# Eleven of 26 convolution groups as float32 tap sums on GpSimd and VectorE, in a dilated attention and gated convolution kernel with a written-out order

## The chip, the cores and the metric

The kernel runs on one core of one Trainium2 chip. The metric is device time in microseconds (us), the median of several runs. A profile of one execution stands beside the times: its span runs from the first to the last instruction, and the execution's own time is a little longer than its span. Engines: PE (TensorE, matmul; PEld is its weight load), DVE (VectorE), ACT (ScalarE), POOL (GpSimd), SP (SyncE, which issues the DMAs).

## The reference, cut to what matters

Sliding attention in two kinds of heads, then a gated unit with a causal convolution of five taps along the sequence:

```python
# attention: 8 batches x 8 heads x 576 positions x 64; heads 0-3: the 32 last positions,
# heads 4-7: every fourth of the 128 last
x = attn_out.transpose(0, 2, 1, 3).reshape(B, S, H * D)        # 8 x 576 x 512
for k in range(K):                                             # K = 5
    gate_pre += conv_w[k][None, None, :] * xp[:, k:k + S, :]   # xp: x with 4 zeros ahead
gate = 1.0 / (1.0 + np.exp(-gate_pre))
out = (gate * (x @ w_val)) @ w_out
```

## The kernel before, in words

Everything is cut into tasks, each a few instructions of one engine. `Plan.add` makes a task with its dependencies and the buffers it holds; `ORDER` (lines 16 to 50) lists all task numbers in the order in which they are emitted, with a letter for the engine (P, A, V, G for GpSimd, S) and, behind it, a number of dummy matmuls ("heat", line 659) to be put ahead of that task. `HOMES` gives the buffer number of each buffer use. Nothing is scheduled at run time: each engine does its tasks in that order, and waits for what it needs from others.

A batch goes through these steps. `Lq`, `Lk`, `Lv` load q, k, v (`p` for the plain heads, `d` for the dilated). `Tq`, `Tk` transpose on PE (lines 401, 464), `Eq`, `Ek` copy out of PSUM to qT and kT (312 on ACT, 314 on DVE, both in the helper `copy`). `S` multiplies the scores (333), `E` takes the exponential on ACT (340), `M` multiplies by the mask on DVE (347), both its inputs in SBUF. `A` multiplies by v (356), `N` divides by the sum on DVE (365, 366). `X` transposes back on PE (428, 488) and `F` copies into xT (312, 314), which holds a pair of batches with channels on the partitions, in four chunks of 128; the plain heads give chunks 0 and 1, the dilated heads chunks 2 and 3. GpSimd (316) casts v to bf16: `U` the dilated v (vn, one cast of 128x1536), `HA` to `HD` the plain v of the first four batches (vw, 2, 3, 3 and 2 casts), and once `Wv` and `Wo` the weights (w_val, w_out), whose float32 copies come in by DMA in the three buffers wt0 to wt2.

The gated unit works on pairs of batches, g = 0 to 3. A pair's 1152 tokens are cut in three blocks of 384 (the middle one spans both batches), in the last pair in four of 288; a block has two halves of two channel chunks, cp = 0 and 1. That makes 26 groups, named by g, block k and cp: group 111 is pair 1, block 1, chunks 2 and 3. Each group has a convolution `C` (line 530: 20 matmuls of 64x64 diagonal weights, one for each of five taps, two chunks and two halves of the partitions, summing in PSUM), the tanh `G` on ACT (540), the value product `V` (548, eight matmuls), and the product `Y` of both on DVE (558) into yT. The convolution of a second chunk of a group exchanges the upper and lower 64 partitions (line 528), and the weights are laid out for that. Output blocks `O` of 128 tokens (577, four matmuls) follow when the products of their tokens are there, `EO` evicts them (584 on ACT, 586 on DVE), `ST` stores them.

GpSimd's casts end with the fp32 weights; after about 70 us it has only three casts of vn left. In `homes` and `run` it is asserted that a buffer isn't used by two tensors at once, in the order as written.

Of the kernel before, what the change touches and what calls it, by code (L numbers as in the profile page):

```python
# [7 lines left out]
FP32 = mybir.dt.float32  # L8
BF16 = mybir.dt.bfloat16
AF = mybir.ActivationFunctionType  # L10
ALU = mybir.AluOpType
# [10 lines left out]
135P 185P 136A 125P 128P 129A 126A 111V 165P 166A 140V 130V 137V 116G 127V 186V 234S 202S 157P 158A 187P 115G
118G 117G 141P 171S 175P 176A 188V 192P 193A 131P 142V 132V 173P 172G 174A 189P 190A 208P 209V 210A 143P 133P
177P 178A 180P 203S 134V 211P 235S 250P 144V 159P 181A 213A 212A 227P 228A 153P 154A 11S 238P 205G 251V 194V
179V 191V 160V 182V 239A 206A 195P 229V 196V 207A 167P 168V 204G 12G 183P 184V 155P 252P 224P 225A 214P 240P
215A 9S 253V 156V 199P 254P 241V 255A 226V 217P 218A 161P 230P 197P 162A 200A 324S 267S 236S 216V 219V 245P
256V 220P 198A 246A 231V 10G 625P 628P 221V 323S 266S 325S 237G 626A 257P 242P 243A 276P 629A 222P 326G 223A
258A 278A 277V 163P 341P 232P 303P 247V 244V 259V 233V 342V 304A 299P 300A 164V 339P 260P 248P 329P 305P 330A
340V 268S 261V 631P 630S 355S 384S 533S 627S 346P 356S 249V 343P 264P 306V 265V 273P 632A 347A 344A 348V 274V
275A 272A 345V 262P 301P 302V 279P 280A 292P 634P 635V 263A 349P 350V 327P 293A 328A 289P 281V 282P 283A 290A  # L30
284V 271G 270G 269G 643P 644A 637P 285P 291V 294V 400P 401V 286V 638A 334P 331P 335A 332A 336V 640P 641A 295P
388P 389A 358P 296V 360A 311P 312A 361P 363A 333V 359V 287P 362V 288V 297P 337P 298A 338V 385S 417S 374P 375A
319P 386S 320A 307P 308A 353P 351P 639S 377P 364P 354V 376V 313P 357S 469S 642S 416S 352A 378A 379V 365A 402P
321P 390P 314V 403V 407P 367P 322V 649P 366V 368A 391A 380P 309P 485P 408A 650A 381V 369V 310V 404P 392P 393A
405A 486V 646P 370P 647A 422P 419P 394V 371V 424V 423A 421A 645S 470S 651S 633S 502S 418S 655P 382P 438P 409V
395P 420A 439A 387G 396A 315P 316A 449P 656A 383V 406V 410P 652P 411V 450A 435P 531S 425P 372P 653A 436A 426A
440V 397V 373V 317P 658P 654S 530S 532S 471S 451P 487P 501S 318V 427V 437V 659A 473P 441P 488A 452V 398P 475P
442V 445P 399V 476A 447P 446A 474A 492P 493A 428P 661P 429A 448V 494V 430V 548P 549V 472G 489P 480P 507P 662A
490A 491V 536P 537V 481A 508A 443P 444V 660S 663S 565S 657S 564S 509A 431P 432V 482V 550P 551A 477P 478A 412P
504P 555P 413A 556A 479V 433P 434V 505A 506A 495P 496V 414P 453P 454A 415V 552P 483P 484V 553A 538P 664P 539A  # L40
523P 510P 511A 524A 520P 521A 676P 570P 665V 497P 567P 677A 569A 568A 554V 557V 571A 636S 461P 462A 522V 525V
572A 534S 667P 463P 503S 498A 666S 648S 455P 535G 670P 671A 526P 464V 668V 456V 527V 566S 673P 558P 682P 559V
674A 672S 669S 678S 583P 586P 587A 584A 499P 588V 683V 500V 457P 458A 465P 466A 513P 585V 459P 460V 528P 589P
529A 514A 590V 679P 680A 691P 573P 540P 541A 576P 574A 577A 685P 515V 512V 692V 686A 516P 681S 684S 687S 517V
467P 591P 518P 605P 468V 519A 597P 606A 601P 578V 575V 592V 543P 602A 688P 579P 542V 544A 598A 580V 599P 689A
545V 603P 581P 582A 600V 546P 694P 547V 604V 695A 697P 698V 609P 593P 560P 562P 561V 563A 610A 594A 595P 675S
696S 690S 699S 703P 700P 704V 596V 701V 607P 608V 706P 709P 611P 612V 705S 702S 693S 621P 617P 710V 613P 622A
711S 707A 708S 715P 712P 716A 618A 713A 614A 615P 616V 714S 619P 623P 721P 722A 718P 719A 620V 624V 727P 717S
723S 720S 724P 728A 725A 729S 726S 730P 731A 732S
"""  # L50

HOMES = "01010210000113130211000021002000132000231120022230241102145110103141020101013010110671123222114010302002121011010121100020122020000113021121100010231011014002232122312230001402035111113121011000001040001271122022114211200220201210102211110120022006000113012301031011031312015002120122131011400020471110130403021302202101000612230101122001201213021121220010101202202400001311141011120300130017102102012110131140321053111213132000031220020210061030221022401013242000210112021202210011202120011203140201100102021003120310041312140112140011020113140211031200110403"
# [17 lines left out]
DEPTH = 5  # L70
NAT = 4
# [31 lines left out]
class Plan:  # L103
# [28 lines left out]
    def run(self):  # L132
# [4 lines left out]
        for word in order:  # L137
# [19 lines left out]
def kernel(  # L157
# [10 lines left out]
    nc = tc.nc  # L168
# [13 lines left out]
    NCH = Dm // 128  # L182
# [39 lines left out]
    conv_w = consts.tile([128, NCH, K], BF16, name="conv_w")  # L222
# [82 lines left out]
    SHIFTS = (("HA", ((1, 0, 64, 64, 0), (1, 64, 64, 0, 1)), 1.0),  # L305
# [196 lines left out]
    def gated(g, xb, w_ready):  # L502
# [3 lines left out]
        for k in range(n_blk):  # L506
# [14 lines left out]
            for cp in range(2):  # L521
                pc, gt, pv = Ten("ps2"), Ten("gate"), Ten("ps2")

                def conv(eng, cp=cp, pc=pc, c0=c0, mov=mov, dst=dst, wd=wd):
                    for kk in range(K):
                        for n in range(2):
                            for hb in range(2):
# [7 lines left out]
                t_c = plan.add(f"C{g}{k}{cp}", (PE,), conv,  # L535
                               deps=[x_done[(b, 2 * cp + n)] for b in last for n in range(2)] + [w_ready["conv"]],
                               tens=[pc, gt, xb], out=pc)

                def th(eng, pc=pc, gt=gt, wd=wd):
                    nc.scalar.activation(out=gate[gt.idx][:, :, 0:wd], in_=ps2[pc.idx][:, :, 0:wd],  # L540
                                         func=AF.Tanh, scale=0.5)
                t_g = plan.add(f"G{g}{k}{cp}", (ACT,), th, deps=[t_c], tens=[pc, gt])

                def val(eng, cp=cp, pv=pv, c0=c0, mov=mov, dst=dst, wd=wd):
                    for n in range(2):
# [163 lines left out]
```

## Time and profile before

| | us |
|---|---|
| median of 3 runs | 174.27 |
| lowest, highest | 173.8, 174.28 |
| the profiled execution, its own time | 173.37 |
| its span | 171.7 |

The profile's rows are read thus. A group of instructions stands as line, engine, operation, out<-in by the program's names, partitions x elements and type, count; behind the bar the busy time in us and the mean ns of one, behind the second bar the idle time of the engine just before them and what ended it. The timeline has start, length, engine, line and operation. A window's row has the stretch and its length, then each engine's busy time with its number of instructions. The view of one line or tile has the shortest, median and longest duration in ns. The chain that ended last is followed back from the last instruction, at each step to what released it.

### The profile page before, as it was taken

To read this page: it belongs to the slowest core of one execution; us is meant where nothing else is said; L and a number is where in the kernel's file an instruction comes from. 1 tells how busy PE (TensorE), PEld (TensorE's weight loads), DVE (VectorE), ACT (ScalarE), POOL (GpSimd) and SP (SyncE) were. 2 spreads that over 40 slices of the span, in tenths; PEclk is the share of its full clock that TensorE was granted. 3 is DMA by queue.
4 is the path that set the end of the run, shared out by engine and by line. 5 is a ranking of instruction groups with operands and counts; after the bars stand their busy time and mean duration, and the time that the engine had idled before them with its cause. 6 is when DMAs were issued, how large, how long until landed. Compare 5 with 4: busy or idle time off the path is not lost.

```text
span 171.7 us, 5752 instructions
## 1 busy us (share of the span) xinstructions
PE 153.0 (89%) x2441; PEld 102.2 (60%) x2460; DVE 121.7 (71%) x243; ACT 108.4 (63%) x182; POOL 44.2 (26%) x82
## 2 busy tenths in 40 slices
PE   6697967888989979899999799989999999999990
PEld 1355654677557546567766567576656577666640
DVE  6549778989899579779788658899368776664220
ACT  2147976198868744798847693888946675242542
POOL 7023998560659427403000000210110000000000
PEclk9999999999999999999999999999999999999999
DMA  4999999999799999999994948969979060333445
GB/s 137 325 355 290 375 370 210 311 374 319 200 383 364 362 269 281 373 353 222 282 328 139 267 115 286 373 165 390 270 202 303 2 244 4 116 119 138 186 165 199
DMA packets 49123, 43.63 MB, mean 254 GB/s; under 512 B 22981, under 2 KB 39365, under 8 KB 49098
## 3 DMA queue, kind: packets, MB, share of 16 engines
q1 hardware_dynamic: 49098, 43.27, 82.2%
q8 instruction: 19, 0.31, 0.7%
q14 instruction: 6, 0.05, 0.1%
HBM read 33.83 MB, written 9.44 MB: 252 GB/s over the span
## 4 chain that ended last, share of the span: by engine, by line
PE 58%; DMA 12%; DVE 11%; ACT 6%; SPq 5%; issue 3%; POOL 3%; ACTq 0%; DVEq 0%; POOLq 0%
PE pu L577 17%; PE pd L548 14%; PE pd L530 9%; DMA qk<-in_k_dram 5%; PE pd L356 5%; DVE et L347 4%; DMA wt<-in_moe_w_out_dram 4%; SPq L281 4%; PE pd L333 4%; DMA qk<-in_q_dram 3%; PE pu L464 3%; POOL w_out L316 3%; PE pd L401 2%; PE pu L488 2%; ACT et L340 2%
## 5 line engine op out<-in xcount | busy, mean ns | idle before, releaser
L340 ACT ACTIVATE et<-pd 128x576 bf16<-128x576 f32 x64 | 39.3, 657 | 10.4 <-PE pd L333 9.3
L347 DVE TENSOR_TENSOR et<-et,mask 128x576 bf16<-128x576 bf16 x64 | 33.9, 557 | 4.7 <-ACT et L340 4.5
L548 PE MATMUL pd<-xT,w_val 128*128 128x384 bf16 (+1 forms) x208 | 34.9, 313 | 0.7 <-DVE xn L366 0.4
L577 PE MATMUL pu<-w_out,yT 128*128 128x512 bf16 x127 | 33.4, 379 | 1.4 <-issue 0.6
L558 DVE SCALAR_TENSOR_TENSOR yT<-gate,pd 128x768 bf16<-128x768 bf16 (+1 forms) x26 | 23.0, 886 | 12.5 <-PE pd L548 8.5
L366 DVE TENSOR_TENSOR xn<-pd,rec 96x768 bf16<-96x768 f32 x32 | 30.5, 954 | 1.1
L316 POOL CAST vn<-vd 128x1536 bf16<-128x1536 f32 x8 | 12.3, 1540 | 70.3 <-DMA vd<-in_v_dram 70.3
L540 ACT ACTIVATE gate<-pd 128x768 bf16<-128x768 f32 (+1 forms) x26 | 19.9, 769 | 10.9 <-DVE yT L558 5.5
L548 PEld LDWEIGHTS <-w_val 128*128 128x128 bf16 x208 | 19.4, 97 | 11.6 <-issue 1.5
L530 PE MATMUL pd<-xT,conv_diag 64*64 64x384 bf16 (+1 forms) x520 | 23.1, 313 | 1.8 <-DVE xT L314 1.1
L584 ACT ACTIVATE osb<-pu 128x512 f32<-128x512 f32 x27 | 16.2, 601 | 11.0 <-PE pu L577 10.7
L577 PEld LDWEIGHTS <-yT 128*128 128x128 bf16 x144 | 12.6, 97 | 13.3 <-issue 1.1
L333 PE MATMUL pd<-qT,kT 64*128 64x96 bf16 x384 | 16.1, 209 | 3.1 <-ACT qT L312 0.9
L530 PEld LDWEIGHTS <-conv_diag 64*64 64x64 bf16 x520 | 15.1, 106 | 6.2 <-issue 2.5
L316 POOL CAST vw<-vp 32x384 bf16<-32x384 f32 (+2 forms) x31 | 16.8, 541 | 7.5 <-DMA vp<-in_v_dram 6.1
L356 PEld LDWEIGHTS <-et 128*128 128x128 bf16 x384 | 14.7, 97 | 6.5 <-DVE et L347 2.5
L464 PE MATMUL pu<-ident,qk 128*128 128x128 bf16 x160 | 14.8, 230 | 3.0 <-DMA qk<-in_k_dram 2.0
L333 PEld LDWEIGHTS <-kT 64*128 64x128 bf16 x384 | 10.1, 96 | 11.5 <-issue 6.3
L464 PEld LDWEIGHTS <-qk 128*128 128x128 bf16 x160 | 10.8, 102 | 7.3 <-DMA qk<-in_k_dram 3.0
L314 DVE COPY xT<-pu 128x576 bf16<-128x576 bf16 x18 | 10.1, 568 | 4.0 <-PE pu L488 3.1
L312 ACT COPY xT<-pu 128x576 bf16<-128x576 bf16 x14 | 8.9, 646 | 6.2 <-PE pu L428 3.6
L365 DVE RECIPROCAL rec<-pd 96x12 f32<-96x12 f32 x32 | 7.1, 223 | 7.6 <-PE pd L356 4.5
(52 smaller groups left out, 146.2 us busy)
## 6 DMA issues: line engine op xcount, KB each, us to landing
out_dram<-osb SPq DMA_DIRECT2D x36, 256.0 KB, 2.7
vd<-in_v_dram SPq DMA_DIRECT2D x8, 768.0 KB, 9.3
qk<-in_k_dram SPq DMA_DIRECT2D x8, 576.0 KB, 7.8
qk<-in_q_dram SPq DMA_DIRECT2D x8, 576.0 KB, 8.0
qk<-in_q_dram SPq DMA_DIRECT2D x6, 640.0 KB, 9.1
qk<-in_k_dram SPq DMA_DIRECT2D x6, 640.0 KB, 8.7
vp<-in_v_dram SPq DMA_DIRECT2D x4, 768.0 KB, 7.9
vp<-in_v_dram SPq DMA_DIRECT2D x4, 576.0 KB, 9.8
```

The lines of the kernel that those rows point to most:

```text
L316: nc.gpsimd.tensor_copy(out_, in_)
L333: nc.tensor.matmul(out=ps2[ps.idx][:, l, QB * jj:QB * jj + QB], lhsT=kT[kt.idx][rb, c:c + 128], rhs=qT[qt.idx][rb, c:c + QB], start=True, ...
L340: nc.scalar.activation(out=et[e.idx][:, 0:2 * HW].rearrange("p (l n) -> p l n", l=2), in_=ps2[ps.idx][:, :, 0:HW], func=AF.Exp, scale=scale)
L347: (nc.vector if eng == DVE else nc.gpsimd).tensor_tensor(out=ev, in0=ev, in1=m, op=ALU.mult)
L356: nc.tensor.matmul(out=ps2[po.idx][:, hf, (2 * jj + l) * DA:(2 * jj + l + 1) * DA], lhsT=et[es[hf].idx][:, c:c + 128], rhs=val(j, l), star ...
L366: nc.vector.tensor_tensor(out=xn[xt.idx][0:QB].rearrange("p (h j) l d -> p h (j l) d", h=2), in0=a[:, :, :, 0:D], in1=rr[:, :, :, None].to ...
L464: nc.tensor.transpose(out=o[:, f:f + 128], in_=a[:, c * RD + 128 * cb:c * RD + 128 * cb + 128], identity=ident)
L530: nc.tensor.matmul(out=dst(ps2[pc.idx][64 * ob:64 * ob + 64, n, 0:wd]), lhsT=conv_diag[rb, 2 * cp + n, kk, :], rhs=mov(2 * cp + n, rb, c0 ...
L540: nc.scalar.activation(out=gate[gt.idx][:, :, 0:wd], in_=ps2[pc.idx][:, :, 0:wd], func=AF.Tanh, scale=0.5)
L548: nc.tensor.matmul(out=dst(ps2[pv.idx][:, n, 0:wd]), lhsT=w_val[:, mc, c * 128:(c + 1) * 128], rhs=mov(mc, slice(0, 128), c0), start=(mc = ...
L558: nc.vector.scalar_tensor_tensor(out=yT[yb.idx][:, 2 * cp:2 * cp + 2, t0:t0 + wd], in0=gate[gt.idx][:, :, 0:wd], scalar=1.0, in1=ps2[pv.id ...
L577: nc.tensor.matmul(out=ps1[po.idx], lhsT=yT[yb.idx][:, c, c0:c0 + 128], rhs=w_out[:, c, :], start=(c == 0), stop=(c == NCH - 1))
```

## The change

A list PCONV names eleven groups: 021, 100, 110, 111, 120, 200, 210, 211, 220, 300, 310. For these there is no `C` on PE and no PSUM buffer. In its place stand three tasks, in float32 in the wt buffers:

- `Ka`: the first chunk, all five taps, on GpSimd or VectorE;
- `Kb`: the second chunk, the first four taps, on either engine;
- `Kc`: the second chunk's last tap, always on VectorE, in two instructions of 64 partitions each, which also exchange the two halves of the partitions.

On GpSimd a part is one multiply into the sum, and then, for each further tap, a multiply into a scratch and an addition of the scratch to the sum. On VectorE each further tap is one fused multiply-add. The sums of `Kb` and the scratch always lie in wt0. The tanh `G` reads the wt buffer. The value product of such a group no longer waits for its convolution. conv_w is kept in float32 instead of bf16.

The order and the buffer numbers are new throughout: the loads' order at the start, where each copy out of PSUM is done, the order of groups and outputs, and the dummy matmuls (31 instead of 16; all but two stand ahead of the transposes, scores and attention products of batch 0). GpSimd's order from the w_out casts on is: Wo1, Wo0, HA3, HC3, Ka100, U4, HD3, U5, Kb111, Ka111, Ka110, Kb120, Ka120, Ka200, U6, Kb210, Ka220, U7, Kb211, Ka211, Kb310, Ka310, Kb300; Ka021 stands before them, between U2 and HC2. VectorE has Kb021, Kb100, Kb110, Kb200, Ka210, Kb220, Ka300 and all Kc. U3 goes to ACT. Of the copies out of PSUM, 21 go from DVE to ACT (11 xT, 5 kT, 5 qT). Behind group 300 the order on PE is: C321, C331, C330, O28, V321, O27, V331, O29, O32, V330, O25, O31, O34, O33, O35; the products of block 0 in the last pair are needed by outputs 27 to 29.

```diff
+PCONV = [[0, 2, 1], [1, 0, 0], [1, 1, 0], [1, 1, 1], [1, 2, 0], [2, 0, 0], [2, 1, 0], [2, 1, 1], [2, 2, 0],
+ [3, 0, 0], [3, 1, 0]]
...
-            if t.load:
+            if t.load and eng == SP:
...
-    conv_w = consts.tile([128, NCH, K], BF16, name="conv_w")
+    conv_w = consts.tile([128, NCH, K], FP32, name="conv_w")
...
-                pc, gt, pv = Ten("ps2"), Ten("gate"), Ten("ps2")
+                slow = [g, k, cp] in PCONV
+                pc, gt, pv = Ten("wt" if slow else "ps2"), Ten("gate"), Ten("ps2")
...
+                ka = Ten("wt")
+
+                def taps(eng, n, c=2 * cp, pc=pc, ka=ka, c0=c0, mov=mov, dst=dst, wd=wd):
+                    acc = dst((wt[ka.idx] if n else wt[pc.idx])[:, 0:wd])
+                    tmp = dst(wt[ka.idx][:, GW:GW + wd])
+                    for kk in range(K - n):
+                        x = mov(c + n, slice(0, 128), c0 + kk - (K - 1))
+                        w = conv_w[:, c + n, kk:kk + 1]
+                        if kk and eng == DVE:
+                            nc.vector.scalar_tensor_tensor(out=acc, in0=x, scalar=w, in1=acc, op0=ALU.mult, op1=ALU.add)
+                            continue
+                        e = nc.vector if eng == DVE else nc.gpsimd
+                        e.tensor_scalar(out=tmp if kk else acc, in0=x, scalar1=w, scalar2=None, op0=ALU.mult)
+                        if kk:
+                            e.tensor_tensor(out=acc, in0=acc, in1=tmp, op=ALU.add)
+
+                def last_tap(eng, c=2 * cp + 1, pc=pc, ka=ka, c0=c0, mov=mov, dst=dst, wd=wd):
+                    for lo, to in ((0, 64), (64, 0)):
+                        nc.vector.scalar_tensor_tensor(
+                            out=dst(wt[pc.idx][to:to + 64, GW:GW + wd]), in0=mov(c, slice(lo, lo + 64), c0),
+                            scalar=conv_w[lo:lo + 64, c, K - 1:K], in1=dst(wt[ka.idx][lo:lo + 64, 0:wd]),
+                            op0=ALU.mult, op1=ALU.add)
...
+                if slow:
+                    t_c = [plan.add(f"K{'ab'[n]}{g}{k}{cp}", (POOL, DVE), lambda e, n=n, taps=taps: taps(e, n),
+                                    deps=c_deps, tens=[pc, gt, xb, ka]) for n in range(2)]
+                    t_c.append(plan.add(f"Kc{g}{k}{cp}", (DVE,), last_tap, deps=t_c[1:], tens=[pc, gt, xb, ka]))
...
-                               deps=[x_done[(b, c)] for b in last for c in range(NCH)] + w_ready["val"] + [t_c],
+                               deps=[x_done[(b, c)] for b in last for c in range(NCH)] + w_ready["val"] + (t_c if not slow else []),
```

More of the change, by code (lines that the diff above doesn't have):

```diff
@@ L22 @@
[L22 to L26, printed above, removed]
@@ new lines @@
+229P 230A 270S 220A 216P 254P 158A 159P 160V 221V 255A 217A 240P 153P 185P 186V 231V 218V 11S 207A 209A 161P
+9S 242P 155P 162A 154A 243A 226P 156V 241A 227A 222P 199P 223V 200A 238S 247P 201P 248A 259P 260A 244P 245A
+269S 268S 224P 228V 232P 202A 261V 272G 12G 256P 257A 169P 10G 249V 225V 246V 650P 258V 168A 651A 233V 170V
+647P 234P 235V 278P 648V 334S 239A 275P 277A 276A 280A 279A 307P 308A 339P1 351P 302V 333S 352V 303V 340A 309P
+310V 262P 263V 653P 654A 349P 250P 251V 284P 337P 350A 285A 163P 286V 281P 164V 338A 266P 282A 283V 267A 264P
@@ L534, in conv @@
                                     start=(kk == 0), stop=(kk == K - 1))
[L535 to L540, printed above, removed]
+                ka = Ten("wt")
[12 more added lines that the diff above has]
+                            e.tensor_tensor(out=acc, in0=acc, in1=tmp, op=ALU.add)
@@ new lines, in last_tap @@
+                def last_tap(eng, c=2 * cp + 1, pc=pc, ka=ka, c0=c0, mov=mov, dst=dst, wd=wd):
[4 more added lines that the diff above has]
+                            op0=ALU.mult, op1=ALU.add)
+                c_deps = [x_done[(b, 2 * cp + n)] for b in last for n in range(2)] + [w_ready["conv"]]
@@ new lines, in gated @@
+                if slow:
+                    t_c = [plan.add(f"K{'ab'[n]}{g}{k}{cp}", (POOL, DVE), lambda e, n=n, taps=taps: taps(e, n),
+                                    deps=c_deps, tens=[pc, gt, xb, ka]) for n in range(2)]
+                    t_c.append(plan.add(f"Kc{g}{k}{cp}", (DVE,), last_tap, deps=t_c[1:], tens=[pc, gt, xb, ka]))
+                else:
+                    t_c = [plan.add(f"C{g}{k}{cp}", (PE,), conv,
+                               deps=c_deps, tens=[pc, gt, xb], out=pc)]
@@ L541, in th @@
+                def th(eng, pc=pc, gt=gt, wd=wd, slow=slow):
+                    a = wt[pc.idx][:, 0:2 * GW].rearrange("p (n t) -> p n t", n=2) if slow else ps2[pc.idx]
+                    nc.scalar.activation(out=gate[gt.idx][:, :, 0:wd], in_=a[:, :, 0:wd],
                                          func=AF.Tanh, scale=0.5)
-                t_g = plan.add(f"G{g}{k}{cp}", (ACT,), th, deps=[t_c], tens=[pc, gt])
+                t_g = plan.add(f"G{g}{k}{cp}", (ACT,), th, deps=t_c, tens=[pc, gt])
```

61 lines of the change are left out of this document (31 added, 30 removed), and 6 rows, old and new, of the table SHIFTS.

## The prediction

> **What bounds the kernel now.** I read the page's busy times first, then busy time by stretches, then the chain that ended last.
>
> ```profile
> PE 153.0 (89%) x2441; PEld 102.2 (60%) x2460; DVE 121.7 (71%) x243; ACT 108.4 (63%) x182; POOL 44.2 (26%) x82
> PEclk9999999999999999999999999999999999999999
> 57.00:80.00 23.00, 20.90 (x342) 13.87 (x347) 17.36 (x33) 15.99 (x28) 7.78 (x11) 1.00 1.02 311
> 80.00:110.00 30.00, 28.26 (x476) 19.61 (x469) 22.21 (x40) 20.44 (x34) 0.82 (x1) 1.00 0.88 249
> 110.00:140.00 30.00, 29.29 (x496) 19.14 (x499) 22.58 (x42) 22.46 (x39) 3.15 (x2) 1.00 0.81 228
> 140.00:172.00 32.00, 27.48 (x353) 17.98 (x354) 13.97 (x23) 12.79 (x22) 0.00 (x0) 0.98 0.37 141
> ```
>
> The columns of the stretches are length, then busy time of PE, PEld, DVE, ACT and POOL, clock, DMA share, GB/s. From 57 us on PE is busy 105.9 of 114.7 us (92%), at full clock; POOL is nearly free there (11.8 us). In that part TensorE sets the time, and the chain of waits says the same:
>
> ```profile
> 69.01 0.76 DVE xT L314
> 79.76 0.97 PE pd L530 x20
> 140.40 1.97 PE pd L530 x60
> 154.22 1.73 PE pu L577 x8
> 155.94 0.98 PE pd L548 x8
> 168.05 0.60 ACT osb L584
> ```
>
> (Start, length, what.) L530 is the convolution: one wide group (384 tokens, 20 matmuls) 0.97 us, three narrow ones (288 tokens) 1.97, so 0.66 each. Four output matmuls (L577) take 0.87, a narrow value group (L548) 0.98. After the last eviction ends (168.65) 3.0 us remain of the 171.7 for the last store.
>
> **What TensorE saves.** Of the eleven groups, one (021) lies before 57 us, where PE is not full. The other ten are eight wide and two narrow: 8 x 0.97 + 2 x 0.66 = 9.1 us on the path. There are 31 dummy matmuls instead of 16, all but two of the 15 new ones early; PE's idle time before 57 us (57 - 47.0 busy = 10 us) covers their 6.5 us (15 x 0.43):
>
> ```profile
> 0.00:16.00 16.00, 12.41 (x120) 6.95 (x121) 10.07 (x48) 6.08 (x9) 4.74 (x14) 1.00 0.91 269
> 16.00:57.00 41.00, 34.62 (x669) 24.64 (x672) 35.55 (x62) 30.63 (x53) 27.69 (x56) 1.00 1.03 325
> L659 PE MATMUL pu<-warm 128*128 128x512 bf16 x9 | 3.9, 569 | 1.6 <-DVE warm L234 1.3 <-ACT kT L312 0.2 <-issue 0.2
> L616 DVE TENSOR_TENSOR conv_diag<-ident,conv_w 128x1280 bf16<-128x1280 bf16 x1 | 1.5, 1492 | 0.0
> ```
>
> Without that cover they cost at most 6.5. The searched order of the first 57 us, where the DMA share is 0.91 to 1.03, I take at nothing, between -3 and +3 us by PE's and DVE's idle time there (10.0 and 11.4); no bytes are added. The float32 conv_w enters one product there, 1.49 us, at worst doubled; the same idle time covers it. If nothing else were late the span would be 171.7 - 9.1 + 0.5 (two late dummies, 0.23 each) = 163.
>
> **What GpSimd and VectorE get.** In the changed program's order GpSimd does 56 wide and 13 narrow multiplies (one tensor in), and 44 wide and 10 narrow additions (two tensors in). VectorE does 7 multiplies, 23 fused multiply-adds for whole parts, and 22 half-partition ones for the last tap.
>
> ```profile
> L316 POOL CAST vn<-vd 128x1536 bf16<-128x1536 f32 x8 | 12.3, 1540 | 70.3 <-DMA vd<-in_v_dram 70.3
> L316 POOL CAST vw<-vp 32x384 bf16<-32x384 f32 x21 | 11.5, 547 | 2.0 <-DMA vp<-in_v_dram 1.0
> L316 POOL CAST vw<-vp x31: 454/508/747, 16.0 to 69.8; 32x384 bf16<-32x384 f32 x21, 64x384 bf16<-64x384 f32 x6, 32x320 bf16<-32x320 f32 x4
> L316 POOL CAST vn<-vd x8: 1465/1470/1694, 12.0 to 123.8; 128x1536 bf16<-128x1536 f32 x8
> 2.08 0.44 POOL L241 TENSOR_SCALAR_AFFINE_SELECT mask<-mask 128x288 bf16<-128x288 bf16 x1
> 2.48 0.44 POOL L239 TENSOR_SCALAR_AFFINE_SELECT mask<-mask 128x288 bf16<-128x288 bf16 x1
> 2.98 0.44 POOL L241 TENSOR_SCALAR_AFFINE_SELECT mask<-mask 128x288 bf16<-128x288 bf16 x1
> ```
>
> The third and fourth rows give min/median/max ns. On GpSimd 384 elements take 0.508 and 1536 take 1.470, so 0.835 ns an element on 0.187 us of fixed time. A **multiply** costs 0.51 wide, 0.43 narrow. An **addition** with two inputs isn't in the trace. From below, it costs no less than one input: 0.51 and 0.43. From above, two one-input operations: 1.01 and 0.85. Reading two streams at the row's rate on one fixed time gives 0.83 and 0.67. I take the middle of these last two, 0.92 and 0.76, since the vw rows give time by elements read and nothing shows the inputs read side by side. The last three rows show dependence: the L241 at 2.98 rewrites what the L239 at 2.48 wrote and starts 0.50 later, though it is busy 0.44; an independent one starts 0.40 later. So 0.07 us go with each dependent step, and nearly every step of a tap sum waits for the one before (multiply into a scratch, add, multiply again).
>
> The Trainium skill, GPSIMD Engine Reference, 3.1 (Elementwise), gives 4497 ns for a two-input fp32 addition of 2048 elements, two operands sharing one read port. As an estimate from that page alone, 843 ns for 384; by it the sum below would be 4 us shorter. No row here shows it.
>
> **The shared lock.** The other cost is that GpSimd and VectorE stop each other:
>
> ```profile
> 27.50 2.46 DVE L347 TENSOR_TENSOR et<-et,mask 128x576 bf16<-128x576 bf16 x3 [0.48 <-ACT et L340]
> 27.59 1.69 POOL L316 CAST vn<-vd 128x1536 bf16<-128x1536 f32 x1
> L347 DVE TENSOR_TENSOR et<-et,mask x64: 441/452/1720, 12.6 to 145.2; 128x576 bf16<-128x576 bf16 x64
> L347 DVE TENSOR_TENSOR et<-et,mask 128x576 bf16<-128x576 bf16 x21 | 13.2, 666 | 2.4 <-ACT et L340 2.4
> L347 DVE TENSOR_TENSOR et<-et,mask 128x576 bf16<-128x576 bf16 x15 | 6.4, 450 | 1.4 <-ACT et L340 1.4
> ```
>
> The fourth row is of 16 to 60 us, with GpSimd busy, the fifth of 113 to 172, with GpSimd nearly idle: 666 against 450 ns for the same mask product of two SBUF tensors, +0.22. The three masks at 27.50 take 2.46 us instead of 1.35, because a vn cast starts under the first and holds the second until it ends; the cast takes 1.69 instead of 1.47, held by the first. The Trainium skill, SBUF — State Buffer, Who interferes with whom, says that a VectorE instruction with two SBUF inputs and a GpSimd one that reads SBUF exclude each other, the second blocking fully. These rows agree.
>
> **The chain on GpSimd.** All tap sums share the scratch tile wt0, so groups stand one behind another. Up to 56.3 us GpSimd casts w_out as before:
>
> ```profile
> 50.82 5.49 POOL L316 CAST w_out<-wt 128x512 bf16<-128x512 f32 x7 [1.68 <-DMA wt<-in_moe_w_out_dram]
> ```
>
> Then come five vw casts (2.8), Ka100 (5 x 0.51 + 4 x 0.92 + 0.5 = 6.7), two vn casts (2.9), two vw casts (1.1) and about 2 of blocking: 72 us. Its data (dilated xT of batch 3) is there at 70 (the 69.01 row). From Kb111 to Kb300, in order, GpSimd has:
>
> - 46 wide and 13 narrow multiplies: 46 x 0.505 + 13 x 0.43 = 28.8
> - 36 wide and 10 narrow additions: 36 x 0.92 + 10 x 0.76 = 40.7
> - 92 dependent steps x 0.07 = 6.4, and two vn casts, 3.0
> - blocking by VectorE: 27 masks x 0.22 = 5.9; 17 fused steps in series and half of 18 last taps at 0.29 (0.22 scaled up by a third, an estimate, for the step's longer time) = 7.5; 0.85 of that, as GpSimd isn't always reading: 11.4
> - turnarounds where GpSimd waits for VectorE's last tap: 3, between 0 and 10.
>
> Together 93.3, so Kb300 ends at 165. Behind it stand Kc300 (2 x 0.45 + 0.2), the tanh (0.65), the product (0.75), then on PE nine outputs and three value groups queued behind output 28, which needs that product: 9 x 0.87 + 3 x 0.98 = 10.8; an eviction 0.60 and the store 3.0: 17.
>
> ```profile
> L558 DVE SCALAR_TENSOR_TENSOR yT<-gate,pd 128x768 bf16<-128x768 bf16 x18 | 17.1, 948 | 6.5 <-PE pd L548 6.4
> L558 DVE SCALAR_TENSOR_TENSOR yT<-gate,pd 128x576 bf16<-128x576 bf16 x8 | 5.9, 748 | 5.9 <-ACT gate L540 3.8 <-PE pd L548 2.1
> L540 ACT ACTIVATE gate<-pd x26: 645/811/866, 21.3 to 161.4; 128x768 bf16<-128x768 f32 x18, 128x576 bf16<-128x576 f32 x8
> ```
>
> The products price the fused step too: 948 ns for 768 and 748 for 576 elements give 1.04 ns an element on 0.15, so 0.55 for 384, 0.45 for 288 (they read one input from PSUM, the taps both from SBUF; the lock is counted apart). **Sum: 165.3 + 17 = 182.3 of span, and 1.7 outside it (the profiled execution took 173.37 for 171.7): 184.** The runs' median, 174.27, is 0.9 above that execution; I leave it in the range.
>
> **Rivals.** *GpSimd keeps up (faster).* If an addition costs 0.51, the 40.7 becomes 22.4 and Kb300 ends at 147; 164 of span by the chain, 163 by TensorE: 166 in all. The point from which it decides: the 10.6 us by which my sum exceeds 173.4, over 44 wide-sized additions, are 0.24 each, so below 0.68 us an addition (blocking as above) the change gains. For it: GpSimd is busy only 4.0 us of the 91.7 from 80 us on. Against: two inputs cost more than one, and the lock.
>
> *VectorE is the bound.* It drops 12.0 us of copies, which go to ScalarE (xT 11 x 0.57, kT 4 x 0.75 and one at 0.45, qT 5 x 0.45), and gets 37 x 0.55 + 8 x 0.45 + 7 x 0.4 (a multiply, between 0.35 and 0.55) = 26.8.
>
> ```profile
> L314 DVE COPY xT<-pu 128x576 bf16<-128x576 bf16 x18 | 10.1, 568 | 4.0 <-PE pu L488 3.1 <-PE pu L428 0.5 <-ACT et L340 0.3
> L314 DVE COPY kT<-pd 128x576 bf16<-128x576 bf16 x6 | 4.5, 754 | 5.6 <-PE pu L428 3.1 <-PE pd L401 2.2 <-ACT kT L312 0.3
> L314 DVE COPY qT<-pu 128x576 bf16<-128x576 bf16 x8 | 3.6, 450 | 1.7 <-PE pu L464 1.4 <-ACT osb L584 0.3
> L312 ACT COPY xT<-pu 128x576 bf16<-128x576 bf16 x14 | 8.9, 646 | 6.2 <-PE pu L428 3.6 <-PE pu L488 2.6
> ```
>
> With waits of 0.4 (half an addition) on 45 fused steps and 6 more on masks it is at 160 us (121.7 - 12.0 + 26.8 + 18 + 6). At 97% busy, with 5 at the start and 8 at the end without it, that is 178 of span, 180 in all: 176 to 184. ScalarE, at 108.4 + 21 copies x 0.65 + a vn cast, stays near 124 and isn't a bound.
>
> *No net change*: additions near 0.68.
>
> **How the numbers follow.** GpSimd's chain 0.50 (own range 176 to 194: additions 0.83 to 1.01 give -4 to +4, blocking and turnarounds 8 to 22 instead of 14, -6 to +8, not all at once); VectorE's queue 0.23; GpSimd keeps up 0.24 (163 to 172.8); no change 0.03. So faster by over 0.3% (about what a measurement of this kernel can tell from no change) 0.24, within it 0.03, slower 0.73. Likeliest 184; the range 165 to 194 takes in both signs.
>
> **What would show it.** Right: GpSimd's additions at 0.8 to 1.0 us and GpSimd almost without idle time from 72 us to 165; masks at 0.6 us or more after 80 us; PE idle waiting for yT's products late; PE busy near 147 us. Wrong: additions below 0.68, masks at 0.45 throughout, Kb300 done before 155. VectorE the bound: GpSimd waits in front of its tap sums while VectorE is over 95% busy.

## The result and the profile after

| | us |
|---|---|
| kernel before, median of 4 runs | 174.06 (173.8 to 174.28) |
| changed kernel, median of 4 runs | 235.75 (235.65 to 235.8) |
| ratio, with its 95% interval | 1.354 (1.352 to 1.357) |
| span of the profiled execution after | 234.0 |

The change costs 61.7 us, where I had forecast 10. From the page of the changed kernel: busy times, GpSimd's and the clock's slices, and the chain that ended last by engine and by line.

```profile
PE 167.6 (72%) x2255; PEld 105.2 (45%) x2255; DVE 152.2 (65%) x273; ACT 121.5 (52%) x205; POOL 189.3 (81%) x204
POOL 5047975999999999999999999999999999998000
PEclk9999999999999999965979799578879995997999
POOL 70%; PE 15%; issue 5%; DVE 3%; DMA 2%; ACT 2%; SPq 1%; POOLq 0%; DVEq 0%
POOL wt L551 40%; POOL wt L553 22%; PE pu L609 3%; POOL vw L319 3%; POOL vn L319 3%; PE pd L580 2%; DMA qk<-in_q_dram 2%; POOL w_out L319 2%; PE pu L467 2%; PE pd L534 2%; PE pd L404 1%; DVE yT L590 1%; PE pd L336 1%; ACT qT L315 1%; PE pd L359 1%
```

GpSimd is at least 90% busy in every slice from the 8th to the 36th (from 41 us on), and 70% of the chain is its work: 40% the multiplications of the taps (L551), 22% the additions (L553). TensorE, 89% busy before, waits. Its groups by line and shape, and VectorE's:

```profile
L551 POOL TENSOR_SCALAR wt<-xT,conv_w 128x384 f32<-128x384 bf16 x56 | 78.7, 1409 | 5.6 <-ACT xT L315 2.3
L553 POOL TENSOR_TENSOR wt<-wt,wt 128x384 f32<-128x384 f32 x32 | 33.5, 1046 | 2.7
L551 POOL TENSOR_SCALAR wt<-xT,conv_w 128x288 f32<-128x288 bf16 x13 | 13.8, 1070 | 0.7
```

```profile
L350 DVE TENSOR_TENSOR et<-et,mask 128x576 bf16<-128x576 bf16 x64 | 38.3, 628 | 3.2 <-ACT et L343 3.1
L548 DVE SCALAR_TENSOR_TENSOR wt<-xT,conv_w,wt 128x384 f32<-128x384 bf16 x19 | 16.0, 842 | 0.7
```

A multiplication takes 1.41 us in the mean, where I had priced 0.51. The additions, which I had thought the doubtful term at 0.92, take 1.05. The timeline shows GpSimd at the casts of w_out, at the start of its long chain, at a quiet moment and at the end (start, length, what):

```profile
58.94 5.26 POOL L319 CAST w_out<-wt 128x512 bf16<-128x512 f32 x7
...
82.86 2.91 POOL L551 TENSOR_SCALAR wt<-xT,conv_w 128x384 f32<-128x384 bf16 x2
...
117.98 0.99 POOL L553 TENSOR_TENSOR wt<-wt 128x384 f32<-128x384 f32 x1
119.07 1.24 POOL L551 TENSOR_SCALAR wt<-xT,conv_w 128x384 f32<-128x384 bf16 x1
...
214.10 1.00 POOL L551 TENSOR_SCALAR wt<-xT,conv_w 128x288 f32<-128x288 bf16 x1
215.19 0.79 POOL L553 TENSOR_TENSOR wt<-wt 128x288 f32<-128x288 f32 x1
```

Kb111 starts at 82.86, Kb300 ends at 215.98; a multiplication that nothing holds takes 1.24, and 18.0 us of tail follow. Who waits for it (line, what for, us in total, times, longest):

```profile
ACT gate L572 <- POOL wt L553: 39.0, 6, 8.7
DVE yT L590 <- ACT gate L572: 23.3, 5, 7.8
PE pd L359 <- POOL vn L319: 11.9, 2, 7.9
```

The tanh waits for the sums, the products of yT for the tanh, and TensorE for casts of v that are queued behind tap sums on GpSimd.

### The profile page after: what moved, and what is told of

It is laid out like the page before. It is cut to its first block, busy times and chain, and to the rows that moved or that the text cites. A ratio compares the mean times of both kernels' runs of the same rounds, so it can differ in the third digit from the quotient of the medians.

```text
span 234.0 us, 5536 instructions
## 1 busy us (share of the span) xinstructions
PE 167.6 (72%) x2255; PEld 105.2 (45%) x2255; DVE 152.2 (65%) x273; ACT 121.5 (52%) x205; POOL 189.3 (81%) x204
## 4 chain that ended last, share of the span: by engine, by line
POOL 70%; PE 15%; issue 5%; DVE 3%; DMA 2%; ACT 2%; SPq 1%; POOLq 0%; DVEq 0%
POOL wt L551 40%; POOL wt L553 22%; PE pu L609 3%; POOL vw L319 3%; POOL vn L319 3%; PE pd L580 2%; DMA qk<-in_q_dram 2%; POOL w_out L319 2%; PE pu L467 2%; PE pd L534 2%; PE pd L404 1%; DVE yT L590 1%; PE pd L336 1%; ACT qT L315 1%; PE pd L359 1%
## 5 line engine op out<-in xcount | busy, mean ns | idle before, releaser
L551 POOL TENSOR_SCALAR wt<-xT,conv_w 128x384 f32<-128x384 bf16 (+1 forms) x69 | 92.5, 1345 | 6.3 <-ACT xT L315 2.3
L609 PE MATMUL pu<-w_out,yT 128*128 128x512 bf16 x144 | 42.7, 432 | 11.7 <-ACT xT L315 5.2
L343 ACT ACTIVATE et<-pd 128x576 bf16<-128x576 f32 x64 | 39.8, 659 | 12.4 <-PE pd L336 12.0
L350 DVE TENSOR_TENSOR et<-et,mask 128x576 bf16<-128x576 bf16 x64 | 38.3, 628 | 3.2 <-ACT et L343 3.1
L553 POOL TENSOR_TENSOR wt<-wt,wt 128x384 f32<-128x384 f32 (+1 forms) x36 | 36.7, 1018 | 3.0
L572 ACT ACTIVATE gate<-wt 128x768 bf16<-128x768 f32 (+1 forms) x11 | 9.0, 819 | 46.5 <-POOL wt L553 39.0
L557 DVE SCALAR_TENSOR_TENSOR wt<-xT,conv_w,wt 64x384 f32<-64x384 bf16 (+1 forms) x22 | 15.9, 724 | 14.0 <-POOL wt L553 13.7
L336 PEld LDWEIGHTS <-kT 64*128 64x128 bf16 x384 | 11.4, 101 | 20.0 <-issue 16.3
L315 ACT COPY xT<-pu 128x576 bf16<-128x576 bf16 x25 | 16.0, 646 | 7.0 <-PE pu L491 3.8
L548 DVE SCALAR_TENSOR_TENSOR wt<-xT,conv_w,wt 128x384 f32<-128x384 bf16 (+1 forms) x23 | 18.6, 809 | 0.8
L553 POOL TENSOR_TENSOR wt<-wt 128x384 f32<-128x384 f32 (+1 forms) x18 | 17.4, 968 | 1.5
L359 PE MATMUL pd<-vn,et 128*128 128x65 bf16 x192 | 9.3, 200 | 11.9 <-POOL vn L319 11.9
```

Source lines behind the costliest of these rows:

```text
L336: nc.tensor.matmul(out=ps2[ps.idx][:, l, QB * jj:QB * jj + QB], lhsT=kT[kt.idx][rb, c:c + 128], rhs=qT[qt.idx][rb, c:c + QB], start=True, ...
L343: nc.scalar.activation(out=et[e.idx][:, 0:2 * HW].rearrange("p (l n) -> p l n", l=2), in_=ps2[ps.idx][:, :, 0:HW], func=AF.Exp, scale=scale)
L350: (nc.vector if eng == DVE else nc.gpsimd).tensor_tensor(out=ev, in0=ev, in1=m, op=ALU.mult)
L359: nc.tensor.matmul(out=ps2[po.idx][:, hf, (2 * jj + l) * DA:(2 * jj + l + 1) * DA], lhsT=et[es[hf].idx][:, c:c + 128], rhs=val(j, l), star ...
L551: e.tensor_scalar(out=tmp if kk else acc, in0=x, scalar1=w, scalar2=None, op0=ALU.mult)
L553: e.tensor_tensor(out=acc, in0=acc, in1=tmp, op=ALU.add)
```

## The experiments

My theory, from the trace: GpSimd's chain is the bound, and what I mis-sized is the multiplication itself. Rivals: the multiplication is slow because VectorE blocks it; the searched order or VectorE's new work costs as much. Beside these kernels the kernel before took 173.47 to 173.59.

**1. What the operations cost alone.** At the end of the kernel before, operations on buffers of their own, one at a time and then against VectorE:

```diff
+        G.tensor_scalar(out=f32[2][:, 0:X], in0=b16[0][:, 0:X], scalar1=cw, scalar2=None, op0=ALU.mult)
+        G.tensor_scalar(out=f32[2][:, 0:X], in0=b16[0][:, 0:X], scalar1=0.5, scalar2=None, op0=ALU.mult)
...
+        G.tensor_tensor(out=f32[2][:, 0:X], in0=b16[0][:, 0:X], in1=cw.to_broadcast([128, X]), op=ALU.mult)
```

> The kernel before, with probes after its last task, alone on their engines: GpSimd's operations one by one at 384 elements (multiply by a pointer scalar and by a constant, bf16 or float32 in, float32 or bf16 out; copies; additions; a product with a broadcast column; memsets), then six of VectorE's fused multiply-adds alone, then ten of them against ten GpSimd additions, against ten multiplies, and against ten memsets. My theory now: the multiply that GpSimd does for a tap costs 1.24 us by itself, not 0.51, and the pointer scalar is what makes it dear; then the multiply by a constant takes about 0.5 and a copy from bf16 to float32 about 0.5. Rival: any tensor_scalar on GpSimd is dear, pointer or constant: both about 1.24. Second rival: the multiply alone is 0.5 and it is VectorE's blocking that makes it 1.4 in the changed kernel: then all multiplies here are about 0.5. An addition alone 1.0. For the lock: against additions or multiplies the fused step, 0.55 alone, takes 1.0 us or more each; against memsets, which read nothing, 0.55.

GpSimd's groups in that kernel, then VectorE's, from 157 us on:

```profile
L688 POOL TENSOR_SCALAR pa<-pb,pw 128x384 f32<-128x384 bf16 x3 | 3.7, 1247 | 0.3
L689 POOL TENSOR_SCALAR pa<-pb 128x384 f32<-128x384 bf16 x3 | 3.5, 1168 | 0.3
L693 POOL TENSOR_SCALAR pa<-pb,pw 128x768 f32<-128x768 bf16 x3 | 6.6, 2203 | 0.0
L694 POOL CAST pa<-pb 128x384 f32<-128x384 bf16 x3 | 1.5, 502 | 0.2
L696 POOL TENSOR_TENSOR pa<-pa,pa 128x384 f32<-128x384 f32 x3 | 3.0, 991 | 0.3
L697 POOL TENSOR_TENSOR pa<-pa,pa 128x768 f32<-128x768 f32 x3 | 5.4, 1799 | 0.2
L698 POOL TENSOR_TENSOR pa<-pb,pw 128x384 f32<-128x384 bf16 x3 | 2.5, 827 | 0.2
L711 POOL TENSOR_SCALAR pa<-pb,pw 128x384 f32<-128x384 bf16 x10 | 13.3, 1329 | 0.8
L707 POOL TENSOR_TENSOR pa<-pa,pa 128x384 f32<-128x384 f32 x10 | 11.7, 1167 | 0.7
L715 POOL MEMSET pa<- 128x768 f32 x10 | 7.4, 737 | 0.5
L700 POOL MEMSET pa<- 128x768 f32 x3 | 2.2, 737 | 0.2
```

```profile
L703 DVE SCALAR_TENSOR_TENSOR pa<-pb,pw,pa 128x384 f32<-128x384 bf16 x6 | 3.7, 619 | 41.3 <-POOL pb L701 41.1
L706 DVE SCALAR_TENSOR_TENSOR pa<-pb,pw,pa 128x384 f32<-128x384 bf16 x10 | 12.4, 1240 | 1.0 <-POOL pb L704 0.7
L710 DVE SCALAR_TENSOR_TENSOR pa<-pb,pw,pa 128x384 f32<-128x384 bf16 x10 | 7.3, 730 | 0.9 <-POOL pb L708 0.6
L714 DVE SCALAR_TENSOR_TENSOR pa<-pb,pw,pa 128x384 f32<-128x384 bf16 x10 | 6.2, 619 | 7.3 <-POOL pb L712 6.9
```

The multiplication takes 1.247 us with VectorE idle, so blocking isn't what makes it slow; by a constant it takes 1.168, so the factor in memory, which I had suspected, isn't either. A cast with the same shapes and types takes 0.502: my row was a true row, but of another operation. The same product, written as a two-input product with the factor's column repeated, takes 0.827. On VectorE the fused step takes 0.619 alone (L703), 0.619 beside memsets (L714), 0.730 beside multiplications (L710) and 1.240 beside additions (L706). So the additions, with two inputs, hold it up most and memsets, which only write, not at all; that a multiplication would cost it as much as an addition, as I had expected, is not so.

**2. The new order without the tap sums.** The changed order, with all eleven groups back on TensorE (the 21 copies stay on ScalarE, the 31 dummy matmuls too).

```diff
-PCONV = [[0, 2, 1], [1, 0, 0], [1, 1, 0], [1, 1, 1], [1, 2, 0], [2, 0, 0], [2, 1, 0], [2, 1, 1], [2, 2, 0],
- [3, 0, 0], [3, 1, 0]]
+PCONV = []
```

> The changed kernel's order, loads, copies on ScalarE and dummy matmuls, but all eleven groups convolved on TensorE again, each just ahead of its tanh. If GpSimd's tap sums make the whole loss, this takes 170 to 178 us. If the new order, or the 21 copies moved to ScalarE, cost a part, 185 or more.

181.39 us, ratio 1.046 (1.041 to 1.050): 7.8 us slower than the kernel before, between what the two theories said. So an order that was searched for one set of prices costs something by itself when the work is put back, but it isn't where the 61.7 us went.

**3. The tap sums on GpSimd cut to one tap.** This leaves four or three of the taps out of each part that GpSimd does.

```diff
-                    for kk in range(K - n):
+                    for kk in range(1 if eng == POOL else K - n):
```

> The changed kernel, but GpSimd's fifteen parts stop after their first tap; the other taps of these parts are left out (54 multiplies and 54 additions). VectorE's parts and all last taps are as they were. If the chain of tap sums on GpSimd sets the time, 165 to 178 us: TensorE's 9 us of savings show at most in part, for VectorE still has its 45 fused steps. If VectorE's queue or ScalarE's is a bound of its own, 180 to 190. If the order is, over 190.

169.88 us in one run. The page's busy times:

```profile
PE 150.8 (90%) x2255; PEld 98.1 (58%) x2255; DVE 138.8 (83%) x273; ACT 119.7 (71%) x205; POOL 65.6 (39%) x96
```

With GpSimd's chain out of the way TensorE is the bound again, 11.5 us below experiment 2; its busy time is 8.9 below (159.7 there). So the saving on TensorE is real, and with sums that cost nearly nothing on GpSimd the whole change, in this order, would be worth 3.7 us.

**4. All parts on VectorE.** In the order every `Ka` and `Kb` gets the letter V; the first seven of fifteen:

```diff
-165G ... 301G ... 318G ... 317G ... 311G ... 324G ... 323G
+165V ... 301V ... 318V ... 317V ... 311V ... 324V ... 323V
```

> The changed kernel, but GpSimd's fifteen parts are done by VectorE as fused multiply-adds, in the same place of the order; nothing is left out. VectorE gets 12 wide and 3 narrow multiplies (7 us) and 44 wide and 10 narrow fused steps (0.55 and 0.45: 29 us), and loses the blocking, some 18 us: about 170 us busy of its own. If GpSimd's rate is the cause, 180 to 195 us. If the cause is that VectorE is full, it gets longer than the changed kernel, over 236.

214.57 us (212.26 to 215.89), ratio 1.232 (1.223 to 1.241): 20 us above the upper end. Its windows (length, busy time of PE, PEld, DVE, ACT, POOL, clock, DMA share, GB/s):

```profile
110.00:140.00 30.00, 21.19 (x256) 13.28 (x253) 28.87 (x53) 18.84 (x33) 1.76 (x1) 0.89 0.48 148
140.00:172.00 32.00, 24.37 (x370) 14.97 (x371) 28.66 (x50) 19.97 (x36) 1.47 (x1) 0.89 0.62 177
```

VectorE is busy 57.5 of 62 us there, so it is the bound in this stretch, though 82% over the span: a share over the span hides that the groups come bunched. What else is in the 20 us was not settled.

**5. The multiplication as a product with a repeated column.** Nothing is left out.

```diff
-                        e.tensor_scalar(out=tmp if kk else acc, in0=x, scalar1=w, scalar2=None, op0=ALU.mult)
...
+                        wb = w.to_broadcast([128, wd]) if len(x.shape) == 2 else w[:, None, :].to_broadcast([128, 2, wd // 2])
+                        e.tensor_tensor(out=tmp if kk else acc, in0=x, in1=wb, op=ALU.mult)
```

> The changed kernel with one edit: GpSimd multiplies by a product of two tensors, the second of which is the weight's column repeated, in place of the multiply by a pointer scalar. The probes gave 0.83 us for it against 1.25. Nothing is left out. If the chain on GpSimd sets the time, 56 wide multiplies get 0.42 shorter and 13 narrow ones some 0.33: 28 us, so 206 to 212 us. If something else is behind the 62 us (the lock by itself, VectorE's queue, the order), it stays above 225.

213.32 us, ratio 1.228 (1.223 to 1.232): 22.4 us come back by this alone, where I expected 28; the time lies 1.3 above that range. A group from GpSimd, one from VectorE, and GpSimd's last instruction:

```profile
L555 POOL TENSOR_TENSOR wt<-xT,conv_w 128x384 f32<-128x384 bf16 x56 | 55.6, 1001 | 5.7 <-DVE rec L368 1.9 <-DVE wt L561 1.2
```

```profile
L350 DVE TENSOR_TENSOR et<-et,mask 128x576 bf16<-128x576 bf16 x64 | 49.5, 803 | 1.3 <-ACT et L343 1.1
```

```profile
192.29 0.89 POOL L557 TENSOR_TENSOR wt<-wt 128x288 f32<-128x288 f32 x1
```

The product takes 1.00 here and 0.83 alone, and masks 0.80 instead of 0.63: by these rows the lock takes part of the gain. The chain ends at 193.18, the span at 211.5.

**6. Three taps instead of five on GpSimd** (two or one are left out of each part there).

```diff
+                    for kk in range(3 if eng == POOL else K - n):
```

> The changed kernel, GpSimd's parts stopping after three taps; what is left out are the fourth and fifth tap of its nine first chunks and the fourth of its six second chunks. From group 111 on that takes 20 wide and 4 narrow pairs of multiply and addition off the chain, 20 x 2.62 + 4 x 2.04 = 61 us at the durations in the changed kernel's trace less what the chain then waits for data: if the time falls one for one until another bound is met, 172 to 182 us. If the loss were spread (by the lock, or the order), about halfway between 170 and 236: 195 to 210.

184.98 us in one run, above the range by 3. GpSimd's last instruction, and the chain that ended last by engine:

```profile
164.12 0.93 POOL L553 TENSOR_TENSOR wt<-wt 128x288 f32<-128x288 f32 x1
DVE 29%; POOL 19%; PE 10%; issue 5%; POOLq 1%; ACT 0%
```

It ends 50.9 us earlier than in the changed kernel, and the span (183.0) is 51.0 shorter: the end still follows the end of GpSimd's chain one for one. But the chain that ended last runs mostly through VectorE up to 135.4 us and through GpSimd only behind that, and VectorE is busy 77.7 of the 83 us from 57 to 140. So 51 us came off, though 61 were left out from group 111 on alone: with GpSimd's work shorter, VectorE is the next bound.

**7. GpSimd as long, but reading nothing.** Multiplications and additions replaced by memsets of the same length, so the sums are left out.

```diff
+                        mul, add = (1413, 1123) if wd == 384 else (1124, 865)
...
+                        e.memset(junk[:, 0:mul], 0.0)
...
+                            e.memset(junk[:, 0:add - (wd + 185 if end else 0)], 0.0)
```

> The changed kernel, where each multiply and addition on GpSimd is a memset of the same length in time (its size from the probes: 0.10 us and 0.83 ns an element), and the last of each part writes the sum; the tap sums of GpSimd's parts are left out. The chain on GpSimd is as long as its operations are alone, but reads no SBUF. If blocking between GpSimd and VectorE makes no more than the excess of GpSimd's durations over the probes (about 12 us), 220 to 226 us, and masks and fused steps take their 0.45 and 0.62. If the lock costs more than that, through VectorE's delays, under 215.

222.05 us in one run, as expected. VectorE's masks and fused steps, and GpSimd's last instruction:

```profile
L351 DVE TENSOR_TENSOR et<-et,mask 128x576 bf16<-128x576 bf16 x64 | 31.7, 523 | 2.7 <-ACT et L344 2.4
L549 DVE SCALAR_TENSOR_TENSOR wt<-xT,conv_w,wt 128x384 f32<-128x384 bf16 x19 | 11.8, 619 | 0.7
```

```profile
202.02 0.34 POOL L561 MEMSET wt<- 128x288 f32 x1
```

Masks fall from 0.63 to 0.52, the fused step from 0.84 to its 0.62 alone, and the time by 13.7 us. That is the most that the lock costs in this kernel, for two other things changed with it: GpSimd no longer waits 2.3 us for xT ahead of Ka021, and the gaps between its dependent steps are 0.05 to 0.07 instead of 0.09 to 0.10. The Trainium skill, SBUF — State Buffer, Who interferes with whom, says that a two-input VectorE instruction contends with GpSimd instructions that read SBUF and not with those that only write it; experiment 1 agrees for additions and memsets (1.240 against 0.619), experiment 7 for memsets (0.619). For multiplications, which read one tensor, the agreement is weak: 0.730 in experiment 1.

**8. Seven groups in the order of before.** Repeated column, first parts on GpSimd, second parts on VectorE but for one group, each part 14 to 20 tasks ahead of the product that needs it.

```diff
+PCONV = [[1, 2, 1], [1, 2, 0], [2, 0, 1], [2, 1, 1], [2, 2, 1], [3, 1, 1], [3, 3, 0]]
```

> A version that may beat both: the order of the kernel before, seven groups (120, 121, 201, 211, 221, 311, 330) as tap sums, those whose product comes 11 us or more behind their data; the first chunk on GpSimd with the repeated-column product (five of 0.83 and four additions of 0.99, 8.8 us a wide part), the second on VectorE, but for 311, whose second chunk is on GpSimd too; each group's tanh just ahead of its product. Nothing is left out. TensorE loses 5 x 0.97 + 2 x 0.66 = 6.2 us; VectorE gets 24 us of work and blocking on top of 122. If GpSimd's chain fits where it has slack, 167 to 171 us. If VectorE's added work in the path of the products decides, 174 to 180.

201.65 us, ratio 1.160 (1.156 to 1.164), a clear miss of both theories. The page's busy times, the chain by engine, and a wait:

```profile
PE 157.6 (79%) x2320; PEld 100.6 (50%) x2320; DVE 156.3 (78%) x281; ACT 108.9 (54%) x182; POOL 105.8 (53%) x152
PE 39%; DVE 34%; issue 7%; ACT 7%; DMA 7%; SPq 4%; DVEq 0%; ACTq 0%
ACT gate L573 <- DVE wt L558: 19.7, 6, 6.3
```

No engine is full and GpSimd isn't on the chain; ScalarE stands 19.7 us at six tanhs. So a sum need not be long in total to cost time. Experiments 9 to 11 ask whether that is a price of each group or of its place.

**9 to 11. Five groups, and two, in the changed order; two in the order of before.** All with the repeated column. In 11 both parts of a group stand on GpSimd, 57 to 70 tasks ahead of the product.

```diff
+PCONV = [[0, 2, 1], [1, 0, 0], [1, 1, 0], [2, 0, 0], [2, 2, 0]]     (9)
+PCONV = [[1, 0, 0], [2, 2, 0]]                                      (10)
+PCONV = [[1, 2, 1], [2, 2, 1]]                                      (11)
```

> The changed kernel's order with five groups (021, 100, 110, 200, 220) on tap sums, GpSimd's multiplications as products with a repeated column, and the other six groups back on TensorE. Theory: a moved group costs only while GpSimd's chain is the last to end. These five put 5 products and 4 additions each on GpSimd, four of them after 57 us, about 4 x 11 = 44 us between 67 and 150 us, which leaves GpSimd idle in between; TensorE is the bound again and the time is that of the order alone less four groups, 181.4 - 4 x 0.97 = 177.5: 175 to 180. Rival: every moved group has a price of its own (lock, waits in the in-order queues), as the line between 181.4 with none and 213.3 with eleven says, 2.9 us a group: 181.4 + 5 x 2.9 = 196, 190 to 200.

> The same with two groups (100 and 220) alone. Theory (only a late chain costs): 181.4 - 2 x 0.97 = 179.5, 178 to 181. Rival (every group has its price): 181.4 + 2 x 2.9 = 187, 185 to 190.

> The order of the kernel before with two of its 26 groups (121 and 221) on tap sums: both parts on GpSimd with the product by a repeated column, started 62 to 66 tasks (about 15 us) ahead of the product that needs them, last tap on VectorE, everything else as before. A group has 9 products and 7 additions on GpSimd, 16 to 18 us. Theory: with the chain early enough TensorE keeps the bound and two groups of 0.97 are saved: 173.6 - 1.9 = 171.7, 171 to 173; if the chains come some us late, each delays the tanh and the product behind it and the gain goes: 173 to 177. Rival (a price for every group): 173.6 + 2 x 2.9 = 179.4, 178 to 181.

Measured: five groups 186.27 (1.072, 1.068 to 1.076), two 181.82 (1.049, 1.044 to 1.054), two in the order of before 180.57 (1.041, 1.037 to 1.044). In the changed order the time goes 181.4, 181.8, 186.3, 213.3 with 0, 2, 5 and 11 groups. A price of 2.9 us for each group, the rival, would have given 187 and 196, and falls in this order. But my theory missed too: two groups lie 0.8 above its range, and five lie 6.3 above theirs; the 4.9 us of five groups above none, where I expected 4 less, show that moved groups cost before the chain on GpSimd is the last to end. Which waits make up those 4.9 was not settled. In the order of before the rival does not fall: run 11 lies in its range of 178 to 181 and outside both of the theory's, and per group the price is 3.6 us there and 4.0 in experiment 8. No run moved the same set of groups in both orders, so how much is the place and how much the group stays open. No version that does all the work beats the kernel before. Run 11 shows how two groups can cost 7.1 us. One line each from the timelines of GpSimd, VectorE, ScalarE and TensorE around the first of them:

```profile
88.14 1.79 POOL L315 CAST vn<-vd 128x1536 bf16<-128x1536 f32 x1
```

```profile
87.36 2.99 DVE L557 SCALAR_TENSOR_TENSOR wt<-xT,conv_w,wt 64x384 f32<-64x384 bf16 x2
```

```profile
90.43 0.84 ACT L572 ACTIVATE gate<-wt 128x768 bf16<-128x768 f32 x1 [3.34 <-POOL vn L315]
```

```profile
91.76 0.43 PE L332 MATMUL pd<-qT,kT 64*128 64x96 bf16 x12 [2.82 <-DVE kT L313]
```

The sums started at 70.60, when GpSimd's casts of v were done, and the last addition ended at 88.2. VectorE's two last taps meet that addition and then the cast of v, and take 2.99 us together; that cast stood at 79.36 before and is 8.8 us late. ScalarE stands 3.34 us at the tanh (the view names the cast, but the tanh begins when the last tap ends), the copies behind it wait in both queues, and TensorE stops for 2.82. At 146.6 the second group does the like: ScalarE stands 2.64. One of this kernel's windows, and its busy times:

```profile
80.00:110.00 30.00, 25.29 (x384) 16.61 (x377) 22.08 (x37) 17.55 (x29) 9.39 (x9) 0.94 0.73 197
PE 155.8 (87%) x2420; PEld 101.6 (57%) x2420; DVE 129.4 (72%) x247; ACT 108.4 (61%) x182; POOL 75.2 (42%) x114
```

TensorE is busy 3.0 us less than before from 80 to 110 (28.26 there). Over the whole span (178.6) it is idle 22.8 us instead of 18.7 and busy 155.8 instead of 153.0, though it does the work of two groups less, at a mean granted clock of 0.988 instead of 0.998: 4.1 and 2.8, together the 6.9 by which the span is longer.

## Why the prediction was wrong, point by point

**The step that failed** is the price of the multiplication: "On GpSimd 384 elements take 0.508 ... A multiply costs 0.51 wide, 0.43 narrow." A cast was taken for any one-input operation. Measured alone it is 1.247 wide, and 1.00 narrow where nothing held it. I had bounded the addition from both sides and kept 0.51 as known; the term that I did not bound was the one that was furthest off. A second term stood at nothing without a reason: GpSimd's start at 72 goes from casts of w_out that end at 56.3, as before, though Ka021 stands ahead of them.

The chain from Kb111 to Kb300 was to take 93.3 us and took 133.1 (215.98 - 82.86). With the prices of experiment 1 and, for narrow operations, the two unheld ones at 214.10 and 215.19:

| term | predicted | measured |
|---|---|---|
| multiplications, 46 wide and 13 narrow | 28.8 | 46 x 1.247 + 13 x 1.00 = 70.4 |
| additions, 36 wide and 10 narrow | 40.7 | 36 x 0.991 + 10 x 0.79 = 43.6 |
| blocking (both groups' busy time in this stretch, 123.7, less the two above) | 11.4 | 9.7 |
| two casts | 3.0 | 3.0 |
| dependent steps and turnarounds (the rest) | 9.4 | 6.4 |
| sum | 93.3 | 133.1 |

(123.7 is 46 x 1.400 + 13 x 1.070 + 36 x 1.037 + 10 x 0.81; the ten wide multiplications ahead of Kb111 are slower and raise the mean of all to 1.409.) The multiplication alone is 41.6 us over; the other terms together are 1.8 under, which makes the 39.8 by which the chain is too long. The start is the other part: 82.9 instead of 72. Ka021 takes GpSimd from 41.16 to 54.19, and the casts of w_out behind it end at 64.2 instead of 56.3: 7.9 of the 10.9. In experiment 2, the same order with Ka021 on TensorE, they end at 56.4, so it is Ka021 that delays them. The other 3.0 arise behind them, where Ka100 takes 11.4 instead of 6.7, with five multiplications at 0.74 over price. 10.9 + 39.8 = 50.7, and the tail gives 1.0 more: 182.3 + 51.7 = 234.0.

**What held:**

- *GpSimd's chain as the bound, and the sign.* The last tap's end and the span:

| kernel | GpSimd's last tap ends | span | difference |
|---|---|---|---|
| changed kernel | 215.98 | 234.0 | 18.0 |
| 5, repeated column | 193.18 | 211.5 | 18.3 |
| 6, three taps | 165.05 | 183.0 | 18.0 |
| 7, no reads | 202.36 | 220.3 | 17.9 |

  I had worked out 17.
- *The addition*, 0.92 taken within 0.51 to 1.01: 0.991. By the doubled length (1.799) it is 2.10 ns an element on 0.18 us. The Trainium skill, GPSIMD Engine Reference, 3.1 (Elementwise), gives 4497 ns for 2048 elements, which I had scaled to 843; scaling without the fixed time was what made that too low, since 2.10 x 2048 + 180 is 4.5 us again.
- *The lock*, 11.4 us on GpSimd, where the busy times leave 9.7 and experiment 7 gives at most 13.7 for the whole kernel. That the two lie so near is in part luck: mine was worked out for a chain 40 us shorter, and with every fused step delayed 0.29, where a multiplication delays it 0.11 and an addition 0.62. VectorE's fused step was priced at 0.55 and is 0.62.
- *The saving on TensorE*, 9.1, or 10.1 with group 021: TensorE's busy time in experiment 3 is 8.9 below that in experiment 2.

**What did not:**

- *The break-even.* I put it at 0.68 us for an addition. With the true multiplication no price of an addition would have brought the gain: at 0.51 and 0.43 the chain from Kb111 would still be 133.1 - 36 x 0.48 - 10 x 0.36 = 112 us and the span about 213, and with additions that cost nothing the span would be 234.0 - 43.6 = 190.
- *VectorE as the bound* (0.23) isn't seen in the changed kernel, at 65%; but with the cheaper product (experiment 5) it is at 84%, and with GpSimd's parts cut to three taps (experiment 6) most of the chain up to 135 us is VectorE's, at 184.98 us. So it stands right behind GpSimd's chain. Experiment 4, with all parts on VectorE, is another split than the rival's, whose 180 no run tests.
- *The order*, which I took at nothing within 3 us up to 57 us and did not price behind that, costs 7.8 with the groups on TensorE.
- *TensorE's busy time*, "near 147", is 167.6, for the same 2255 matmuls as the 150.8 of experiment 3. The mean granted clock is 0.905 against 0.969, which goes the right way; how much of the 16.8 it makes was not settled, for experiment 6 has 153.4 at 0.989. The last section has the clock's windows.

## What to carry to other kernels

A one-input row prices only its own operation: before work is moved to an engine, look whether the trace has that very operation there, and if not, keep a wide bound on it, above all on the term with the largest count. Work moved off a busy engine onto an idle one must end before its consumer's turn in an in-order queue, not just fit into idle time in total; in experiment 11 two tanhs that stood about 3 us each came with a loss of 7. And the most that the move can gain should be measured first, with the moved work cut to almost nothing: here, in the searched order, it was 3.7 us.

## What the runs showed of the hardware

- On GpSimd a multiplication by one factor for each partition takes 1.247 us for 384 elements and 2.203 for 768 (2.49 ns an element), a cast 0.502, a two-input addition 0.991, and the two-input product with a repeated column 0.827. The one-input form is the dearest of these.
- Memsets on GpSimd and VectorE's two-input steps leave each other alone (0.737 and 0.619 both alone and together); two-input additions do not (0.991 becomes 1.167, 0.619 becomes 1.240). One-input multiplications lie between, though they read too: 1.247 becomes 1.329, with the fused steps over after about half of them, and 0.619 becomes 0.730.
- In the changed kernel the clock that TensorE is granted is lower where it idles more. From its windows (columns as above), and the longest wait of its weight loads:

```profile
57.00:80.00 23.00, 18.14 (x302) 12.33 (x302) 20.12 (x31) 15.64 (x26) 21.48 (x26) 1.00 1.04 357
80.00:110.00 30.00, 19.88 (x321) 13.26 (x321) 21.65 (x34) 17.94 (x32) 28.49 (x25) 0.85 0.64 171
140.00:172.00 32.00, 17.41 (x225) 11.04 (x221) 16.88 (x25) 13.80 (x24) 30.38 (x26) 0.79 0.62 177
200.00:234.00 34.00, 23.39 (x231) 13.45 (x229) 15.62 (x25) 8.89 (x15) 14.91 (x16) 0.95 0.28 108
PEld L359 <- issue: 23.1, 10, 8.2
```

  It is 1.00 while TensorE is busy 79% of the time, and 0.79 where it is busy 54%. The Trainium skill, TensorE: Matmul & The Clock Gate, HAM oscillation, warns of idle gaps over about 3.4 us; the rows agree in direction, with waits of up to 8.2 us in the last line. No run varied the gaps alone, so the threshold isn't shown here.
